# Up-projection bank by bank, and rounding, sine and gate of two banks one after the other in second halves

## The chip, the cores and the metric

The kernel runs on one core of one Trainium2 chip. The metric is the device time of one execution in microseconds; smaller is better. Of the engines, TensorE (PE) multiplies matrices into PSUM banks, VectorE (DVE), ScalarE (ACT) and GpSimd (POOL) work on tiles, and the SyncE queue (SP) issues most of the DMAs; ScalarE's queue issues a few.

## The reference

Two blocks, one behind the other. The first is an mLSTM cell over 4 batches, 8 heads, 768 steps and head size 40; the second takes its output as 3072 rows of 320 and computes `x @ w_in` (320 by 2048), then `h * cos(h)`, then a product with `w_out` (2048 by 320).

```python
for t in range(S):
    m_new = np.maximum(f_gate[:, :, t] + m, i_gate[:, :, t])
    f_stab = np.exp(f_gate[:, :, t] + m - m_new)
    i_stab = np.exp(i_gate[:, :, t] - m_new)
    m = m_new
    C = f_stab[:, :, None, None] * C + i_stab[:, :, None, None] * np.einsum('bhd,bhe->bhde', vt, kt)
    n = f_stab[:, :, None] * n + i_stab[:, :, None] * kt
    h_tilde = np.einsum('bhde,bhe->bhd', C, qt)
    denom = np.maximum(np.abs(np.einsum('bhd,bhd->bh', n, qt)[:, :, None]), 1.0)
    y[:, :, t] = h_tilde / denom / (1.0 + np.exp(-o_gate[:, :, t]))
...
h = x @ w_in
return ((h * np.cos(h)) @ w_out).astype(np.float32)
```

## The kernel before

The sequence is cut into 6 chunks (c) of 128 steps. A cell n = 4c + b is chunk c of batch b, with all 8 heads: 24 cells, n = 0 to 23. In a cell the scores (matrices k by q, line 485) are weighed by the decay on VectorE (`weigh`, 491), multiplied by the values (`values`, 511 to 520), normalised on VectorE (`normalize_turned`, 529 to 540; the last step writes `xT`, the input of the second block), and the state is brought up to date (`seam`, 603, puts the increments in PSUM; `state`, 628, adds them on VectorE in four instructions, two for each half of the partitions; `fade`, 586, on POOL; cells 20 to 23 have no such update). `seam_out` (610) copies the last 64 of the 320 features, which a cell leaves in `xT`, into `xL` by two DMAs that ScalarE's queue issues. The transposes of q and k for the next cell are two VectorE instructions (`turn_blocks`, 458), and the next scores wait for them; `scale_q` (467) and `weigh_k` (413) prepare further operands on POOL.

The second block works on a chunk whose cells are done. Its 2048 columns of `w_in` are taken in 8 parts (f2 = 0 to 7) of 256 columns, called halves here, since two of them go with one cell. `Up` (633) makes one: it takes two PSUM banks of 128 by 512 float32 (`pup`), one for each 128 columns (e = 0, 1), and fills each by three products: two of 128 rows (line 651) and one of 64 rows (line 645, `low`, from `xL`). The pool `ps_u` has two banks in all, so a half may write a bank only when the half before has finished reading it. In odd f2 of chunks 0 to 4 `low` is issued first, otherwise last. Then come four steps for each bank: `near` (659, ScalarE) rounds to int32, `rest` (662, VectorE) takes the remainder, `sin` (667, ScalarE) takes the sine of it, `gate` (671, VectorE) multiplies the sine by the bank. The result `g` goes to `sums` (720 to 723 on VectorE, 725 to 728 on POOL), which prepares a product with fewer multiplications, and that product with `w_out` is issued in `down_slot` (line 761, tiles `acc` and `late`; in chunk 0 line 683, tile `po`). At the second half that goes with the first cell of a chunk (n = 12, 16, 20), VectorE also has `combine` and `combine_late` (781 to 798) for the output of the chunk before.

The order is written out by hand, in one program order that every engine keeps for its own instructions (`manual_schedule`). `both_parts(c, b)` (966) issues a cell n = 4(c + 1) + b together with two halves of chunk c: the first (i = 0, even f2) with the scores ahead and `weigh` between `rest` and `sin`, then `down_slot`, `values`, `seam`, `normalize_turned`; the second (i = 1, odd f2) with `seam_out`, `state`, `sums`, then `down_slot`, and the preparations for cell n + 1. In chunk 5 there are halves but no cells. The first cells, 0 to 3, have an order of their own (`first_cells`).

In chunk 0 the weights are also converted, from 64-bit numbers to float32, between these steps: `take_apart` (154, 156) on ScalarE, `bound` (160, 161) and the first part of `put_together` (167) on VectorE, its last part (168) on POOL. A buffer of raw weights is free for the next load, issued on SP, only when its last step is done.

In second halves the order on ScalarE before was: near of both banks, the two DMA issues of `seam_out`, sine of both banks; and on VectorE: rest of both banks, the four instructions of `state`, gate of both banks, `sums`, the transposes.

Of the kernel before, what the change touches and what calls it, by code (L numbers as in the profile page):

```python
# [29 lines left out]
def kernel(  # L30
# [33 lines left out]
    NK = DM // 128  # L64
# [317 lines left out]
    def psum_o():  # L382
        return ps_o.tile([128, HP, C], FP, name="pm", tag="o")
# [6 lines left out]
    def decay_exponents(n):  # L390
        E = Es[n]
        if n < B:
            nc.vector.tensor_tensor(out=E, in0=E, in1=cols(n, 0, C), op=OP.subtract)
        nc.gpsimd.affine_select(out=E, in_=E, compare_op=OP.is_ge, fill=1.0e30, base=0,
                                pattern=[[0, H], [1, C]], channel_multiplier=-1)
# [45 lines left out]
    def clear_low():  # L441
        for w in "qk":
            nc.gpsimd.memset(raws[w][1], 0.0)
# [34 lines left out]
    def scores(n):  # L478
        pool, tag = psum(n)
        qT, kT = qkT[n]  # L480
        ps = [pool.tile([128, HP, C], FP, name="ps", tag=tag) for _ in range(2)]
        for p in range(HP):
            for j in range(2):
                r = slice(64 * j, 64 * j + D)
                nc.tensor.matmul(ps[j][:, p], kT[r, p], qT[r, p], start=True, stop=True)  # L485
        pss[n] = ps

    def weigh(n):
        for j in range(2):
            w = Es[n].rearrange("p (a j) t -> p a j t", j=2)[:, :, j]  # L490
            nc.vector.tensor_tensor(out=w, in0=pss[n][j], in1=w, op=OP.mult)  # L491
# [51 lines left out]
    def new_x(c):  # L543
        xT[c] = p2.tile([128, NK * B + 1, C], FP, name="xT", tag="xT")
        xL[c] = p2.tile([128, B, C], FP, name="xL", tag="xL")
# [20 lines left out]
    def halves(n):  # L566
        for j in range(2):
            r = slice(64 * j, 64 * j + D)
            for lo, hi, x in ((0, 32, HP * 32 * j), (32, DV, H * 32)):
                s = st[n % B][r, x:x + HP * 32].rearrange("q (p d) -> q p d", p=HP)  # L570
                yield j, r, s if lo == 0 else s[:, :, 16 * j:16 * j + 16], slice(lo, hi)

    def increment(n, r, w):
        u = pus[n][r, :, w]
        return u if w.start == 0 else u.rearrange("q p (o d) -> q p d o", o=2)

    def like(s, u):
        return s.rearrange("q p (d o) -> q p d o", o=2) if len(u.shape) == 4 else s
# [27 lines left out]
    def seam_out(n):  # L606
        c, b = divmod(n, B)
        if n >= B:
            for e in range(2):
                nc.scalar.dma_start(out=xL[c][64 * e:64 * e + 64, b], in_=ys[n][0:128:2])  # L610
            return
        if b == 0:
            new_x(c)
        nc.scalar.copy(out=xT[c][:, NK * b:NK * b + NK], in_=pxs[n][:, 0:NK])
        if b == B - 1:
            nc.vector.tensor_copy(out=xL[c][:, b], in_=pxs[n][:, NK])
        else:
            nc.scalar.copy(out=xL[c][:, b], in_=pxs[n][:, NK])

    def state(n):  # L620
        if n < N - B:
            for j, r, s, w in halves(n):
                u = increment(n, r, w)
                s = like(s, u)
                if n < B:
                    nc.scalar.copy(out=s, in_=u)
                else:
                    nc.vector.tensor_tensor(out=s, in0=s, in1=u, op=OP.add)
# [4 lines left out]
    class Up:  # L633


        def __init__(self, c, f2):
            self.c, self.f2 = c, f2
            self.pu = [ps_u.tile([128, B * C], FP, name="pup", tag="up") for _ in range(2)]

            ahead = f2 % 2 == 1 and c < NC - 1  # L640

            def low():
                for e, pu in enumerate(self.pu):
                    r = slice(64 * e, 64 * e + 64)
                    nc.tensor.matmul(pu, w_in_l[r, f2], xL[c][r].rearrange("p b t -> p (b t)"), start=ahead, stop=not ahead)  # L645

            if ahead:
                low()
            for i in range(NK):
                for e, pu in enumerate(self.pu):  # L650
                    nc.tensor.matmul(pu.rearrange("p (b t) -> p b t", b=B), w_in_sb[:, i, ts(2 * f2 + e, 128)], xT[c][:, i:NK * B:NK],  # L651
                                     start=(i == 0 and not ahead), stop=(i == NK - 1 and ahead))
            if not ahead:
                low()
            self.n = [p3.tile([128, B * C], I32, name="n", tag="n") for _ in range(2)]
# [174 lines left out]
    def warm(k, bank=None):  # L830

        for _ in range(k):
            nc.tensor.matmul(bank or pw, nil, nil.unsqueeze(1).to_broadcast([128, HP, 128]), start=True, stop=True)
# [132 lines left out]
    def both_parts(c, b):  # L966

        n = (c + 1) * B + b
        cell = n < N
        for i in range(2):  # L970
            f2 = 2 * b + i
            up = Up(c, f2)
            if cell and i == 0:
                scores(n)
                if c == 0 and b == 0:

                    warm(8, psum_o())
            if cell and i == 1:
                if n % 2 == 1 and n > B + 1 and n + 3 < N:
                    load_two(n + 3, "Kv")  # L980
            for e in range(2):
                up.near(e)
            for e in range(2):
                up.rest(e)
            if i == 0:
                if cell:
                    weigh(n)
                    if n + 1 < N:
                        decay_exponents(n + 1)
                    if n == B:  # L990
                        clear_low()
                for e in range(2):
                    up.sin(e)
                    up.gate(e)
                if c > 0:
                    sums(c, f2)
                if b == 0 and c == 1:
                    sigmoid(c + 1)

                if c == 0:  # L1000
                    next_out(*[pieces.pop(0) for _ in range(min(b, len(pieces), 1))])
                if cell and n + 1 < N:
                    decay(n + 1)
            else:
                if cell:
                    seam_out(n)
                if cell:
                    state(n)
                for e in range(2):
                    up.sin(e)  # L1010
                    up.gate(e)
                if c > 0:
                    sums(c, f2)
                if n == B + 1:
                    low_dimensions(n + 1)
                if c == 0:
                    next_out(*pieces)
                    pieces.clear()
                if cell and n + 1 < N:
                    if c > 0:  # L1020
                        weigh_k(n + 1)
                    odd_values(n + 1)
            if i == 1 and b == B - 1 and 0 < c < NC - 2:
                sigmoid(c + 2)
                sin_next()
            down_slot(c, f2)
            if f2 == 0 and c > 1:
                for p in range(2):
                    combine_first(c - 1, p)
            if cell and i == 0:  # L1030
                turn_gate(n)
                values(n)
                seam(n)
                normalize_turned(n)
                fade(n)
                if c == 1 and b < 3:
                    weight_sums(b + 1)
                if n % 2 == 1 and n > B + 1 and n + 3 < N:
                    load_two(n + 3, "qk")
                if n > B + 1 and n + 3 < N:  # L1040
                    load_E(n + 3)
                if b == B - 2 and c + 2 < NC:
                    load_o(c + 2)
                if c == 0 and pieces:
                    to_float32(pieces.pop(0))
                sin_next()
            if f2 == 0 and c > 1:
                for p in range(2):
                    combine(c - 1, p)
            if i == 1:  # L1050
                if c == 0 and b + 2 < B:
                    pieces.extend(weights_in(b + 2))
                    load_two((n + 3) // 2 * 2)
                    load_E(n + 3)
                if cell and n + 1 < N:
                    turn_blocks(n + 1)
                    scale_q(n + 1)
                    if c == 0:
                        weigh_k(n + 1)
                if (c, f2) == (0, LAST):  # L1060
                    weight_sums(0)
# [43 lines left out]
```

## Time and profile before

| | |
|---|---|
| time, median of 3 runs | 542.03 us (541.94 to 544.99) |
| span of the profiled execution | 541.8 us |
| TensorE busy | 518.0 us (96%) |
| VectorE busy | 420.1 us (78%) |
| ScalarE busy | 285.1 us (53%) |
| POOL busy | 227.0 us (42%) |
| mean granted TensorE clock | 0.980 of full speed |

The profile records one execution; its span runs from the first to the last instruction. A busy share is an average over stages with different limits: the first 50 us or so (first cells, loads), chunk 0 with the conversion of weights (to about 147 us), chunks 1 to 4 (to about 465 us), and chunk 5 with the last products. Costliest groups (busy in all, and one instruction):

| line | engine | what | number | busy us | one, ns |
|---|---|---|---|---|---|
| 651 | PE | pup, 128 rows | 384 | 178.4 | 607 |
| 645 | PE | pup, 64 rows | 192 | 54.3 | 642 |
| 659 | ACT | near | 96 | 53.6 | 593 |
| 662 | DVE | rest | 96 | 62.9 | 687 |
| 667 | ACT | sine | 96 | 57.7 | 628 |
| 671 | DVE | gate | 96 | 61.6 | 683 |

A float32 product is two instructions in the trace, here called passes, and the mean of one includes the overlap with its neighbours; from one start to the next of the 128-row passes is about 0.44 us. In the rows of a timeline, x2 says that two instructions are merged in one row, and the bracket gives the engine's idle time before it and what ended it.

### The profile page before, as it was taken

What the parts mean: (1) busy time and instruction counts of PE and PEld (TensorE: products, weight loads), DVE (VectorE), ACT (ScalarE), POOL (GpSimd) and SP (SyncE); (2) the same over time, 40 slices, a digit from 0 to 9 for tenths busy, and PEclk for the clock granted to TensorE, in tenths of its full rate; (3) what the DMA queues carried; (4) which work ended last, traced back from release to release, by engine and by line L of the source; (5) the groups of instructions that cost most, each with busy time, mean ns of one, the idle gap of its engine ahead of it and who ended that gap; (6) DMA issues with size and microseconds to landing.
All of it is one profiled execution on the core that took longest, in us unless ns stands there. A gap on an engine that the chain in (4) does not pass through costs nothing.

```text
span 541.8 us, 10496 instructions
## 1 busy us (share of the span) xinstructions
PE 518.0 (96%) x3844; PEld 349.5 (65%) x3844; DVE 420.1 (78%) x907; ACT 285.1 (53%) x546; POOL 227.0 (42%) x369
## 2 busy tenths in 40 slices
PE   7997889879999999999999999999999999999996
PEld 4874545545566666766767757757757767576755
DVE  5864978689688897898887898888898878673636
ACT  2876938496395355836436836526836522222221
POOL 7535354446376665434443533543422421221211
PEclk9968889999999999999999999999999999999999
DMA  9999759489677737519439329249320000010001
GB/s 137 209 199 222 220 151 214 131 164 246 137 124 178 104 94 168 63 68 208 46 95 189 41 82 198 44 107 178 38 93 7 2 5 6 10 41 1 0 1 48
DMA packets 99940, 57.81 MB, mean 107 GB/s; under 512 B 62305, under 2 KB 92609, under 8 KB 99889
## 3 DMA queue, kind: packets, MB, share of 16 engines
q1 hardware_dynamic: 96496, 55.64, 48.3%
q10 hardware_dynamic: 3248, 1.33, 1.2%
q8 instruction: 30, 0.49, 0.4%
q14 instruction: 22, 0.17, 0.1%
q0 software_dynamic: 144, 0.18, 0.1%
HBM read 51.71 MB, written 4.11 MB: 103 GB/s over the span
## 4 chain that ended last, share of the span: by engine, by line
PE 75%; DVE 9%; DMA 7%; POOL 2%; SPq 2%; ACT 2%; issue 2%; DVEq 0%; POOLq 0%; ACTq 0%
PE pup L651 27%; PE acc L761 23%; PE pup L645 8%; PE po L683 3%; PE ps L485 3%; PE late L761 3%; DMA E<-M_d 2%; PE vt L520 2%; DMA bits<-in_moe_w_in_dram 2%; PE vt L511 2%; DMA xL<-xT 1%; PE pu L603 1%; DVE g L671 1%; DMA vs<-in_v_dram 1%; SPq L330 1%
## 5 line engine op out<-in xcount | busy, mean ns | idle before, releaser
L651 PE MATMUL pup<-xT,w_in_sb 128*128 128x512 f32 x384 | 178.4, 607 | 5.2 <-DVE g L671 2.5
L659 ACT ACTIVATE n<-pup 128x512 int32<-128x512 f32 x96 | 53.6, 593 | 194.1 <-PE pup L645 142.6
L651 PEld LDWEIGHTS pup<-xT,w_in_sb 128*128 128x128 f32 x384 | 70.3, 192 | 93.0 <-issue 88.1
L662 DVE SCALAR_TENSOR_TENSOR n<-pup,n 128x512 f32<-128x512 f32 x96 | 62.9, 687 | 80.1 <-ACT n L659 78.7
L725 POOL TENSOR_TENSOR D<-g 128x128 f32<-128x128 f32 x40 | 19.9, 497 | 218.2 <-DVE g L671 218.2
L667 ACT ACTIVATE n<-n 128x512 f32<-128x512 f32 x96 | 57.7, 628 | 23.1 <-DVE n L662 15.4
L671 DVE SCALAR_TENSOR_TENSOR g<-pup,n 128x512 f32<-128x512 f32 x96 | 61.6, 683 | 3.9 <-ACT n L667 3.3
L761 PE MATMUL acc<-w_out_sb,g 128*128 128x160 f32 x320 | 58.6, 304 | 0.0
L761 PE MATMUL acc<-T,g 128*128 128x160 f32 x320 | 58.0, 301 | 0.1
L645 PE MATMUL pup<-xL,w_in_l 64*128 64x512 f32 x192 | 54.3, 642 | 1.3 <-POOL w_in_l L168 1.3
L761 PEld LDWEIGHTS acc<-w_out_sb,g 128*128 128x128 f32 x320 | 47.7, 190 | 5.6 <-issue 4.2
L761 PEld LDWEIGHTS acc<-T,g 128*128 128x128 f32 x320 | 48.1, 190 | 3.7 <-issue 3.0
L408 ACT ACTIVATE E<-E,tab 128x128 f32<-128x128 f32 x160 | 49.0, 389 | 0.3
L683 PE MATMUL po<-w_out_sb,g 128*128 128x320 f32 x128 | 36.4, 437 | 1.5 <-POOL w_out_sb L168 1.5
L761 PE MATMUL acc<-T,S 128*128 128x160 f32 x160 | 35.0, 300 | 0.0
L485 PEld LDWEIGHTS ps<-t,t 40*128 40x128 f32 x384 | 24.6, 188 | 12.5 <-DVE t L458 6.6
L683 PEld LDWEIGHTS po<-w_out_sb,g 128*128 128x128 f32 x128 | 23.8, 190 | 13.4 <-POOL w_out_sb L168 3.1
L645 PEld LDWEIGHTS pup<-xL,w_in_l 64*128 64x128 f32 x192 | 14.6, 186 | 25.1 <-issue 19.8
L491 DVE TENSOR_TENSOR E<-ps,E 128x512 f32<-128x512 f32 x48 | 30.6, 679 | 0.0
L761 PE MATMUL acc<-w_out_sb,S 128*128 128x160 f32 x160 | 28.8, 299 | 0.0
L958 ACT ACT_TABLE_LOAD x22 | 28.2, 1283 | 0.4
L761 PEld LDWEIGHTS acc<-T,S 128*128 128x128 f32 x160 | 26.2, 190 | 3.0 <-issue 3.0
(175 smaller groups left out, 878.8 us busy)
## 6 DMA issues: line engine op xcount, KB each, us to landing
E<-M_d SPq DMA_DIRECT2D x22, 512.0 KB
qr<-in_q_dram SPq DMA_DIRECT2D x36, 160.0 KB
kr<-in_k_dram SPq DMA_DIRECT2D x36, 160.0 KB
G<-G_d SPq DMA_DIRECT2D x20, 256.0 KB
bits<-in_moe_w_out_dram SPq DMA_DIRECT2D x8, 640.0 KB
bits<-in_moe_w_in_dram SPq DMA_DIRECT2D x32, 128.0 KB
out_dram<-o_sb SPq DMA_DIRECT2D x24, 160.0 KB
ks<-in_k_dram SPq DMA_DIRECT2D x10, 320.0 KB
```

What stands on the lines that cost most here:

```text
L408: nc.scalar.activation(out=Es[n][:, h], in_=Es[n][:, h], func=AF.Exp, scale=-1.0, bias=tab[:, c, 0, g:g + 1])
L485: nc.tensor.matmul(ps[j][:, p], kT[r, p], qT[r, p], start=True, stop=True)
L491: nc.vector.tensor_tensor(out=w, in0=pss[n][j], in1=w, op=OP.mult)
L645: nc.tensor.matmul(pu, w_in_l[r, f2], xL[c][r].rearrange("p b t -> p (b t)"), start=ahead, stop=not ahead)
L651: nc.tensor.matmul(pu.rearrange("p (b t) -> p b t", b=B), w_in_sb[:, i, ts(2 * f2 + e, 128)], xT[c][:, i:NK * B:NK], start=(i == 0 and not ...
L659: nc.scalar.activation(out=self.n[e], in_=self.pu[e], func=AF.Copy, bias=0.25)
L662: nc.vector.scalar_tensor_tensor(out=self.n[e].bitcast(FP), in0=self.pu[e], scalar=0.25, in1=self.n[e], op0=OP.add, op1=OP.subtract)
L667: nc.scalar.activation(out=r, in_=r, func=AF.Sin, scale=TWO_PI_DOWN)
L671: nc.vector.scalar_tensor_tensor(out=g, in0=self.pu[e], scalar=TWO_PI, in1=self.n[e].bitcast(FP), op0=OP.mult, op1=OP.mult)
L683: nc.tensor.matmul(po[c][b], gs[c, f][:, ts(b, C)], w_out_sb[:, f], start=(f == 0), stop=(f == NF - 1))
L761: nc.tensor.matmul(a, lhs, rhs, start=start, stop=stop)
L958: nc.scalar.activation(out=spot, in_=spot, func=AF.Sin)
```

## The change

Two edits. In `Up` the loops are exchanged: both 128-row products of the first bank are issued ahead of those of the second, in all halves. In `both_parts`, near and rest of both banks are now issued together only in first halves. In second halves `seam_out` comes first, then near, rest and sine of the first bank, near of the second, half of `state`, gate of the first bank, rest and sine of the second, the other half of `state`, gate of the second. `state` takes an argument for it that picks one half. The instructions are the same ones; on ScalarE the order becomes: two DMA issues, near, sine, near, sine; on VectorE: rest, two of `state`, gate, rest, two of `state`, gate. POOL and SP keep their order.

```diff
-    def state(n):
+    def state(n, only=None):
         if n < N - B:
             for j, r, s, w in halves(n):
+                if only not in (None, j):
+                    continue
                 u = increment(n, r, w)
...
-            for i in range(NK):
-                for e, pu in enumerate(self.pu):
+            for e, pu in enumerate(self.pu):
+                for i in range(NK):
                     nc.tensor.matmul(pu.rearrange("p (b t) -> p b t", b=B), w_in_sb[:, i, ts(2 * f2 + e, 128)], xT[c][:, i:NK * B:NK],
                                      start=(i == 0 and not ahead), stop=(i == NK - 1 and ahead))
...
-            for e in range(2):
-                up.near(e)
-            for e in range(2):
-                up.rest(e)
             if i == 0:
+                for e in range(2):
+                    up.near(e)
+                for e in range(2):
+                    up.rest(e)
                 if cell:
                     weigh(n)
...
             else:
                 if cell:
                     seam_out(n)
+                up.near(0)
+                up.rest(0)
+                up.sin(0)
+                up.near(1)
                 if cell:
-                    state(n)
-                for e in range(2):
-                    up.sin(e)
-                    up.gate(e)
+                    state(n, 0)
+                up.gate(0)
+                up.rest(1)
+                up.sin(1)
+                if cell:
+                    state(n, 1)
+                up.gate(1)
                 if c > 0:
                     sums(c, f2)
```

## The prediction

> **What bounds the kernel now.** I read the page's engine row and chain of waits, then the timelines of TensorE, VectorE and ScalarE over one cell of chunk 2, then the waits, then the stages before and after. The chain:
>
> ```profile
> PE 75%; DVE 9%; DMA 7%; POOL 2%; SPq 2%; ACT 2%; issue 2%; DVEq 0%; POOLq 0%; ACTq 0%
> ```
>
> From 126 to 526 us it runs through matmuls almost alone; before that, through weight loading and VectorE; after it, through the last half's rounding, sine and gate. So the price of the change is the TensorE idle time that it makes or removes. One cell (n = 14), TensorE, then VectorE, then ScalarE (start, length, what):
>
> ```profile
> 273.33 3.70 PE L651 MATMUL pup<-xT,w_in_sb 128*128 128x512 f32 x8
> ...
> 280.67 3.60 PE L651 MATMUL pup<-xT,w_in_sb 128*128 128x512 f32 x8
> 284.20 1.13 PE L645 MATMUL pup<-xL,w_in_l 64*128 64x512 f32 x4
> 285.16 1.06 PE L485 MATMUL ps<-t,t 40*128 40x128 f32 x16
> ```
>
> ```profile
> 275.26 0.56 DVE L540 TENSOR_TENSOR xT<-yt,db 128x384 f32<-128x384 f32 x1
> 276.90 1.49 DVE L662 SCALAR_TENSOR_TENSOR n<-pup,n 128x512 f32<-128x512 f32 x2 [1.08 <-ACT n L659]
> 278.31 0.86 DVE L628 TENSOR_TENSOR st<-st,pu 40x128 f32<-40x128 f32 x4
> 279.20 1.29 DVE L671 SCALAR_TENSOR_TENSOR g<-pup,n 128x512 f32<-128x512 f32 x2
> ...
> 282.96 1.07 DVE L458 STREAM_TRANSPOSE t<-kr 128x512 f32<-128x512 f32 x1
> ```
>
> ```profile
> 276.27 0.60 ACT L659 ACTIVATE n<-pup 128x512 int32<-128x512 f32 x1 [3.01 <-PE pup L651]
> 277.07 0.60 ACT L659 ACTIVATE n<-pup 128x512 int32<-128x512 f32 x1 [0.20 <-PE pup L651]
> 277.13 1.18 ACTq L610 DMA_DIRECT2D xL<-xT  x2
> 278.35 1.15 ACT L667 ACTIVATE n<-n 128x512 f32<-128x512 f32 x2 [0.69 <-DMA E<-M_d]
> ```
>
> See: TensorE has no gap. VectorE works without a gap from 276.90 to the end of the transposes, 284.03. The scores (L485), which need them, start at 285.16: 1.07 us of slack after 0.06 us of passing on. That slack is 1.37 in chunk 0's last cell, 0.6 in chunk 1, 1.07 in chunks 2 and 3, 0.64 in chunk 4, and 0 where combine runs (n = 12, 16, 20; transposes end 244.98, scores 245.03). A sine queued behind seam_out's DMA issues waits for them.
>
> **Part 1, product bank by bank.** Same instructions. A pass is 0.44 us (eight in 280.67 to 284.20). In second halves of chunks 0 to 4 the first bank is complete two passes (0.88) sooner, the second as now. In first halves, and in chunk 5, the 64-row products come last and nothing is complete sooner; but the second bank is first written 1.77 after the first, instead of 0.88, so it can be released 0.88 later. One loss: in half 2 of chunk 0 TensorE does four passes, then waits for the second weight block (72.63, idle 2.48, POOL L168). Now two are done and six remain: +0.88.
>
> **Part 2, seam_out ahead of near(0).** On ScalarE the two DMA issues (1.12 to 1.18) now stand before both roundings, and wait for xT (275.82). Nearest row: the one above, where the sine starts 0.04 after the issues end. So near(0) starts about 275.82 + 1.22 = 277.04: not 0.88 sooner (275.39), but 0.77 later than now. Bounds: 275.39 if the issue holds nothing back; 0.95 more if it lasts 2.07, as at 396.76. I take 1.22, the common length.
>
> **Part 3, one bank after the other.** ScalarE and VectorE now hand over in turn: near 0.60, rest 0.69, sine 0.62, gate 0.68, then rest, sine, gate of the second bank 0.69 + 0.62 + 0.68, with 0.17 of passing on: 4.75 from near(0) to the last gate, 4.12 from the first rest. The second rounding runs under the first gate. state's two pairs (0.43 each) lie under the sines: free. Last gate: 277.04 + 4.75 = 281.79, now 280.49: +1.30 (call it d). The first gate ends at 279.73, now 279.85: no gain. Behind the last gate on VectorE wait the sums and both transposes, behind those the scores. TensorE's second bank is needed only at 280.67 + 1.77 = 282.44: no wait (in chunk 1 by 0.2 to 0.3, at n = 20 0.2 too late, where the scores wait longer anyway). POOL's sums come d later too, ahead of weigh_k and scale_q; scale_q's output, ready at 285.03, is read at 290.39: covered. The order on POOL and SP is as it was; SP's q and k loads wait for the transposes, and what they bring is read a cell later or more. state ends some 1.8 later than 279.17; its PSUM tile is free before the scores need one.
>
> The same sum elsewhere (end of L540 + 5.97, against the last gate now) gives d = 1.21, 1.63, 1.64, 1.19 in chunk 1; 1.11 to 1.33 in chunks 2 and 3; 1.34 and 1.96 in chunk 4. In the combine cells VectorE is busy until the first rest, which hides part 2: 237.42 + 4.12 = 241.54 against 240.80, d = 0.74; in chunk 4, without state's 0.86 to save, 398.65 + 4.12 against 401.32, d = 1.45.
>
> **The sum, cells 8 to 23.** Let p be TensorE's lateness. VectorE's lateness x in a cell is p at its first-half product, or p at its scores less the 0.3 to 0.7 by which the normalisation (L529) now starts after the values end (0 at n = 21), if more. The next scores are late by x + d − slack, or by p if that is more. From zero at the scores of cell 8:
> chunk 1: 0.63, 1.16, 1.68, 1.76;
> chunk 2 (0.74 with no slack, then d about equal to the slack): 2.42, 2.42, 2.64, 2.64;
> chunk 3: 3.38, 3.38, 3.63, 3.63;
> chunk 4 (1.45 with no slack): 5.08, 5.78, 6.45.
> So +6.45.
>
> **Chunk 0.** Here weights are converted behind the sines:
>
> ```profile
> 72.63 3.49 PE L651 MATMUL pup<-xT,w_in_sb 128*128 128x512 f32 x4 [2.48 <-POOL w_in_sb L168]
> 95.26 3.67 PE L651 MATMUL pup<-xT,w_in_sb 128*128 128x512 f32 x8 [1.19 <-DVE g L671]
> 100.21 1.13 PE L645 MATMUL pup<-xL,w_in_l 64*128 64x512 f32 x4 [1.28 <-POOL w_in_l L168]
> 121.47 3.67 PE L651 MATMUL pup<-xT,w_in_sb 128*128 128x512 f32 x8 [1.34 <-DVE g L671]
> ```
>
> n = 4: near(0) is held by the table load anyway. The last sine ends 64.95 + 0.69 + 0.03 + 0.62 + 0.03 + 0.68 + 0.69 + 0.03 + 0.62 = 68.34, now 66.82. ScalarE's six conversion steps follow, VectorE's put_together and POOL's L168 come 1.37 later, and TensorE with part 1's 0.88 is 2.24 late. The next weight DMAs wait on SP for POOL's w_out_sb (issue 61.28, length 14.49), so they land 1.37 later too. n = 5: near(0) at 93.24 on that clock; first rest 93.82; the last sine 97.2, now 94.27: +2.95, passed through ScalarE, VectorE and POOL to w_in_l and the transposes (no slack: 101.53, 101.59). n = 6: the same adds 1.1: 4.1. n = 7: d 0.70 under 1.37: nothing. The 1.19 and 1.34 of gate wait shrink, but TensorE then waits for w_in_l and the scores. So +4.1; if the weights landed when they do now, +2.2.
>
> TensorE's idle stretch at 72.63 becomes about 4.9 us (69.2 to 74.0). An idle 3.88 before 55.63 is followed by a granted clock of 0.72 over 56 to 62, a loss of some 1.7 us. Here 1.8 more would be absorbed, since TensorE waits for w_in_l until +2.9 in the next cell. The Trainium skill, TensorE: Matmul & The Clock Gate, "What's actually happening", has the clock halve after an idle window of about 3.4 us. By that rule the sum gains nothing if the wait absorbs it, and an estimated 1.7 if not; the trace agrees with the rule after 3.88 us.
>
> **The tail.** Last half: near(0) 527.66, so the last gate ends 527.66 + 4.75 = 532.41 plus 0.05, now 531.05: +1.41, on the path, since the last 18 matmuls start 0.05 after L723 (533.26). Chunk 5's other second halves lie under 9 us of matmuls.
>
> Total: 4.1 + 6.45 + 1.41 = 12.0 on the span of 541.8, which stands 0.2 under the runs' median of 542.03: 554.0.
>
> **Rivals.**
> Issues hold nothing back: part 2 is free, near(0) starts 0.88 sooner, d is −0.34 in ordinary cells. Left are 3.9 in chunk 0, 0.74 + 0.74 + 1.45 in the combine cells, and the tail: +8.2, 550. For: near(1) at 277.07 and the issue at 277.13 run side by side. Against: the issue is ahead in program order now, and the sine behind it waited.
> Issues last 2.07, as once: 0.95 more in some eight cells (n = 5, 6, 8 to 11, 21, 22): 561.5. For: loads are in flight beside them. Against: 1.12 in nearly all cells.
> Clock lost in chunk 0 and not absorbed: 555.7.
> Not slower: the gate waits of n = 5 and 6 (1.19 + 1.34) go, since the first bank is released 0.55 sooner and the second needed 0.88 later; the tail's 1.41 stays: 540.7. It decides if ScalarE's weight steps end no later than now. Against: they stand behind the last sine, 1.1 to 1.5 later, and the slack of the scores is short in chunk 1.
> That the order stays as it was is excluded: the built instructions stand as the change says.
>
> **How the numbers follow.** Forecast 0.62, hidden issues 0.15, long issues 0.10, clock 0.05, not slower 0.08. Leaving out the last and the outer part of the long issues, the range is 547 (hidden issues, weights landing as now, 2.0 less, and 1 for the hand-overs) to 560. A percent is 5.4 us, about what a measurement here tells from no change. Slower by more: the first four less 0.03 at their low edge, 0.89; within: 0.09; faster: 0.02.
>
> **What would show it.** Right: L610 ahead of L659, near(0) 1.2 after L540; gates one by one, each behind its sine; new TensorE idle before L485 from transposes, 0.5 a cell in chunk 1 and 1.4 at n = 21; the wait for the second weight block in half 2 ending 1.4 later; tail +1.4. Wrong: near(0) at the first bank's end, L485 without idle, or weights converted at the old times.

## The result, and the profile after

The changed kernel takes 556.55 us in the median of 4 runs (554.37 to 558.52); the kernel before, on the same chip, 541.99 (541.86 to 544.99, 4 runs). The ratio is 1.0244, with a 95% interval of 1.0208 to 1.0279. The profiled run of the changed kernel took 555.36 us, its span is 553.6. So 1.8 us lie outside the span, and the same 1.7 to 1.9 lie there in nearly every run of every kernel of this study, the kernel before among them.

Lines behind 626 have moved by 2: near is L661, rest L664, sine L669, gate L673, the sums L722 to L725. First the engine row and the chain of waits of the changed kernel:

```profile
PE 524.9 (95%) x3844; PEld 351.5 (63%) x3844; DVE 420.6 (76%) x907; ACT 285.7 (52%) x546; POOL 227.0 (41%) x369
...
PE 52%; DVE 25%; ACT 10%; DMA 4%; issue 3%; SPq 2%; POOL 2%; ACTq 1%; DVEq 0%; POOLq 0%
```

TensorE's share of the chain has fallen from 75% to 52%, VectorE's has grown from 9% to 25% and ScalarE's from 2% to 10%: the hand-over between the two now sets the time of some stages. The waits say the same (engine, tile and line, whom it waits for: us in total, times, the longest):

```profile
ACT n L669 <- DVE n L664: 49.8, 71, 1.8
...
DVE g L673 <- ACT n L669: 22.1, 52, 0.8
...
PEld ps L485 <- DVE t L458: 18.6, 18, 2.5
...
PE ps L485 <- DVE t L458: 5.8, 9, 1.7
```

The waits of the sine on the remainder were 15.4 us before, those of the gate on the sine 3.3. Only the last line is lost time of TensorE: 5.8 us in nine places, where it was 1.1 in three. The line above it is for the same scores, but counts weight loads, which partly run beside earlier products.

The cell of n = 14 in the changed kernel, VectorE's timeline (start, length, what, in brackets the idle time before it):

```profile
279.58 0.56 DVE L540 TENSOR_TENSOR xT<-yt,db 128x384 f32<-128x384 f32 x1
282.03 0.69 DVE L664 SCALAR_TENSOR_TENSOR n<-pup,n 128x512 f32<-128x512 f32 x1 [1.89 <-ACT n L661]
...
283.42 0.69 DVE L673 SCALAR_TENSOR_TENSOR g<-pup,n 128x512 f32<-128x512 f32 x1 [0.38 <-ACT n L669]
284.02 0.68 DVE L664 SCALAR_TENSOR_TENSOR n<-pup,n 128x512 f32<-128x512 f32 x1
...
285.40 0.69 DVE L673 SCALAR_TENSOR_TENSOR g<-pup,n 128x512 f32<-128x512 f32 x1 [0.23 <-ACT n L669]
...
288.55 1.09 DVE L458 STREAM_TRANSPOSE t<-kr 128x512 f32<-128x512 f32 x1
```

and ScalarE's:

```profile
280.18 1.12 ACTq L610 DMA_DIRECT2D xL<-xT  x2
281.40 0.60 ACT L661 ACTIVATE n<-pup 128x512 int32<-128x512 f32 x1 [3.83 <-PE pup L653]
282.75 0.63 ACT L669 ACTIVATE n<-n 128x512 f32<-128x512 f32 x1 [0.76 <-DVE n L664]
283.29 0.58 ACT L661 ACTIVATE n<-pup 128x512 int32<-128x512 f32 x1
284.74 0.63 ACT L669 ACTIVATE n<-n 128x512 f32<-128x512 f32 x1 [0.87 <-DVE n L664]
```

xT is ready at 280.14, the two DMA issues follow, and the first near starts at 281.40: 1.26 later, though the page gives TensorE as its releaser. TensorE's eight passes start at 277.64 and take 3.70, so the first bank was complete before xT; what ended the wait was the issues. From there to the end of the last gate at 286.09 it is 4.69. VectorE, which had no gap here, now idles 2.50 us in this stretch.

TensorE's own timeline, rows picked: chunk 0, the scores of n = 21 and what follows them, the last products:

```profile
71.79 5.48 PE L653 MATMUL pup<-xT,w_in_sb 128*128 128x512 f32 x6 [5.62 <-POOL w_in_sb L168]
...
101.14 2.08 PE L647 MATMUL pup<-xL,w_in_l 64*128 64x512 f32 x4 [2.85 <-POOL w_in_l L168]
...
413.25 1.16 PE L485 MATMUL ps<-t,t 40*128 40x128 f32 x16 [1.72 <-DVE t L458]
414.34 0.81 PE L763 MATMUL acc<-w_out_sb,g 128*128 128x160 f32 x4
414.99 0.67 PE L763 MATMUL acc<-T,S 128*128 128x160 f32 x2
415.45 1.27 PE L763 MATMUL acc<-T,g 128*128 128x160 f32 x4
416.52 1.27 PE L763 MATMUL acc<-w_out_sb,S 128*128 128x160 f32 x4
...
544.11 0.54 PE L763 MATMUL acc<-T,S 128*128 128x160 f32 x2 [0.67 <-DVE S L723]
545.10 0.81 PE L763 MATMUL acc<-T,g 128*128 128x160 f32 x4 [0.46 <-DVE g L725]
```

The gate waits of chunk 0 (1.19 and 1.34) are gone, 0.27 at 65.07 apart. The wait for the second weight block has grown from 2.48 to 5.62, that for w_in_l from 1.28 to 2.85, and after both TensorE is slow: six passes in 5.48, where six at 0.44 would take about 2.7, and four small ones in 2.08 instead of 1.13. (In the kernel before, the four passes after the wait of 2.48 were slow as well: 3.49, at a granted clock of 0.50.) New is the wait of 1.72 at n = 21, with four products in 1.27 behind it instead of 0.71. Where the time was lost, against the kernel before: the first row is taken at the end of n = 4's last write of `xT`, just ahead of the first changed second half (the scores of n = 4 start at nearly the same time in both, 48.91 and 48.86), the later rows at the start of each cell's scores.

| stretch | lateness gained, us | prediction |
|---|---|---|
| first cells, to `xT` of n = 4 | -2.12 | 0 |
| chunk 0, to the scores of n = 8 | 3.96 | 4.1 |
| chunk 1, to n = 12 | 1.88 | 1.76 |
| chunk 2, to n = 16 | 0.91 | 0.88 |
| chunk 3, to n = 20 | 1.03 | 0.99 |
| chunk 4, to n = 23 | 4.67 | 2.82 |
| tail | 1.48 | 1.41 |
| sum, the difference of the spans | 11.8 | 12.0 |

The first cells differ by up to 3.6 us between the profiles here, so lateness below is counted from this write of `xT` in n = 4. One value stands out, chunk 4.

### The profile page after: what moved, and what is told of

Its sections match the earlier page's. It is cut to its first block, busy times and chain, and to the rows that moved or that the text cites. A ratio compares the mean times of both kernels' runs of the same rounds, so it can differ in the third digit from the quotient of the medians.

```text
span 553.6 us, 10495 instructions
## 1 busy us (share of the span) xinstructions
PE 524.9 (95%) x3844; PEld 351.5 (63%) x3844; DVE 420.6 (76%) x907; ACT 285.7 (52%) x546; POOL 227.0 (41%) x369
## 4 chain that ended last, share of the span: by engine, by line
PE 52%; DVE 25%; ACT 10%; DMA 4%; issue 3%; SPq 2%; POOL 2%; ACTq 1%; DVEq 0%; POOLq 0%
PE pup L653 18%; PE acc L763 17%; PE pup L647 5%; DVE n L664 4%; DVE g L673 4%; DVE t L458 4%; ACT n L669 3%; PE ps L485 3%; PE po L685 2%; ACT n L661 2%; PE vt L520 2%; PE vt L511 1%; PE late L763 1%; DVE S L723 1%; DVE S L724 1%
## 5 line engine op out<-in xcount | busy, mean ns | idle before, releaser
L653 PE MATMUL pup<-xT,w_in_sb 128*128 128x512 f32 x384 | 180.5, 612 | 5.9 <-POOL w_in_sb L168 5.6
L661 ACT ACTIVATE n<-pup 128x512 int32<-128x512 f32 x96 | 54.3, 591 | 183.8 <-PE pup L647 117.0
L664 DVE SCALAR_TENSOR_TENSOR n<-pup,n 128x512 f32<-128x512 f32 x96 | 63.8, 685 | 71.5 <-ACT n L661 71.5
L669 ACT ACTIVATE n<-n 128x512 f32<-128x512 f32 x96 | 59.6, 630 | 49.8 <-DVE n L664 49.8
L673 DVE SCALAR_TENSOR_TENSOR g<-pup,n 128x512 f32<-128x512 f32 x96 | 64.0, 687 | 22.1 <-ACT n L669 22.1
L685 PE MATMUL po<-w_out_sb,g 128*128 128x320 f32 x128 | 37.6, 449 | 0.0
L485 PE MATMUL ps<-t,t 40*128 40x128 f32 x384 | 28.0, 287 | 5.9 <-DVE t L458 5.8
```

The costliest lines, as they stand in the source:

```text
L661: nc.scalar.activation(out=self.n[e], in_=self.pu[e], func=AF.Copy, bias=0.25)
L664: nc.vector.scalar_tensor_tensor(out=self.n[e].bitcast(FP), in0=self.pu[e], scalar=0.25, in1=self.n[e], op0=OP.add, op1=OP.subtract)
L669: nc.scalar.activation(out=r, in_=r, func=AF.Sin, scale=TWO_PI_DOWN)
L673: nc.vector.scalar_tensor_tensor(out=g, in0=self.pu[e], scalar=TWO_PI, in1=self.n[e].bitcast(FP), op0=OP.mult, op1=OP.mult)
L685: nc.tensor.matmul(po[c][b], gs[c, f][:, ts(b, C)], w_out_sb[:, f], start=(f == 0), stop=(f == NF - 1))
```

## The experiments

Each is measured against the kernel before on the same chip: 542.51 for seam_between, banks_only, order_only and chunk0_as_before, 541.97 for seam_front, tail_as_before, fill_21 and fill_chunk0, 542.59 for fill_weights, seam_late and seam_late_b.

**seam_between**: the changed kernel with the DMA issues behind the second near.

```diff
-                if cell:
-                    seam_out(n)
                 up.near(0)
                 up.rest(0)
                 up.sin(0)
                 up.near(1)
+                if cell:
+                    seam_out(n)
```

> The changed kernel with one move: in second halves seam_out's two DMA issues go behind near(1), where ScalarE waits for the second remainder anyway. Theory (the DMA issues ahead of near(0), and the one-by-one hand-over, both push the transposes and so the scores): near(0) starts some 2.1 us sooner after xT's last write (from 1.25 after it to the end of the first bank), the waits of the scores in chunk 1 (0.36, 0.37, 0.21) go, those at n = 13 and 17 stay near 0.7, n = 21 stays over 1.4, the tail stays. About 552.3 us, 4 less than the changed kernel's 556.5. Rival (the hand-over alone carries the loss, the issues are hidden): 556.5, chunk 1's waits stay. Rival (it gives everything back): 542.

Measured: 552.79 us (552.45 to 554.05), ratio 1.0187 (1.0162 to 1.0211), 3.8 less than the changed kernel. ScalarE in the cell of n = 14:

```profile
281.01 0.60 ACT L661 ACTIVATE n<-pup 128x512 int32<-128x512 f32 x1 [2.15 <-PE pup L653]
282.37 0.63 ACT L669 ACTIVATE n<-n 128x512 f32<-128x512 f32 x1 [0.76 <-DVE n L664]
282.75 0.47 ACTq L610 DMA_DIRECT2D xL<-xT  x1
282.90 0.58 ACT L661 ACTIVATE n<-pup 128x512 int32<-128x512 f32 x1
```

The issue at 282.75 starts beside the sine and the second near, and here it holds neither back: behind a running instruction it is hidden, ahead of the first one it is not. Chunks 1 to 4 cost 2.90 instead of 8.49; chunk 1 costs 0.20. Not all of the 5.59 is the issues' price: 1.67 of it is the lower clock behind the wait at n = 21 (fill_21 below), which did not come in this profile, though the wait is there (1.73). What is left is three steps of 0.65, 0.68 and 1.36, one for each combine cell (the scores of n = 13, 17, 21). That is the price of the alternation where VectorE is late into the first rounding.

**banks_only**: the kernel before with the loop exchange alone.

```diff
-            for i in range(NK):
-                for e, pu in enumerate(self.pu):
+            for e, pu in enumerate(self.pu):
+                for i in range(NK):
```

> The kernel before with the exchanged product loops alone. Theory: no loss outside chunk 0. In half 2 of chunk 0 six passes instead of four follow the wait for the second weight block, 0.9 us, and up to 2.7 if the longer idle stretch lowers the granted clock; the next cell's wait for w_in_l (1.28 before) takes up most of it: 542 to 543.5 us. Rival (the bank order is a cost of its own, as the product is the bulk of TensorE's work): a third or more of the loss, 547 us or more.

Measured: 544.49 us (541.15 to 545.18, 10 runs), ratio 1.0017 (0.9996 to 1.0037): no difference that can be told from none, though the median is 1.0 above the range expected. In its profile the wait for the second weight block is 3.46 instead of 2.48, with its six passes in 4.39, the gate wait of 1.19 has shrunk to 0.64, and no lateness is gained from n = 8 on.

**order_only**: the changed kernel with the old order of the products; near, rest, sine and gate as changed.

```diff
-            for e, pu in enumerate(self.pu):
-                for i in range(NK):
+            for i in range(NK):
+                for e, pu in enumerate(self.pu):
```

> The changed kernel with the product loops as before (both banks in turn), all else as changed. Theory: the second bank is needed 0.88 us sooner than with bank by bank, so the late second gate now also holds back the first-half product: new waits of 0.3 us a cell in chunks 2 and 3 and 0.8 to 1 in chunks 1 and 4 ahead of L651: 559 to 563 us, slower than the changed kernel. Rival (bank order makes no difference once the scores wait for the transposes): 556.5. Rival (bank by bank is part of the loss): below 555.

Measured: 560.51 us (557.92 to 563.06), ratio 1.0324 (1.0282 to 1.0366). TensorE's timeline in chunks 1 and 2:

```profile
189.73 2.81 PE L653 MATMUL pup<-xT,w_in_sb 128*128 128x512 f32 x6 [0.89 <-DVE g L673]
...
291.59 2.81 PE L653 MATMUL pup<-xT,w_in_sb 128*128 128x512 f32 x6 [0.25 <-DVE g L673]
```

Two passes run, then the second bank is awaited from the late last gate. Bank by bank it is needed two passes later, and these waits do not appear: alone the loop exchange is worth nothing, beside the new order it saves 4.0.

**seam_front**: the kernel before with only the DMA issues moved ahead of both nears.

```diff
+            if cell and i == 1:
+                seam_out(n)
             for e in range(2):
                 up.near(e)
...
             else:
                 if cell:
-                    seam_out(n)
-                if cell:
                     state(n)
```

> The kernel before, with only seam_out's DMA issues put ahead of both roundings in second halves; all else as before. Counted as the prediction counts it: near(0) starts 1.22 after xT, both rests follow, then state, then both gates; the last gate 0.78 later than before in ordinary cells, which the slack of the scores (1.07, 0.6 in chunk 1 and 0.64 in chunk 4) mostly hides. So 2 to 3 us more than the kernel before, 544.5 to 545 us. Rival (the issues cost the same in either order, 3.7, which is what moving them back saved in the changed kernel): 546.2. Second rival (the issues hold nothing back without the alternation): 542.5.

Measured: 547.29 us (546.75 to 548.3), ratio 1.0085 (1.0053 to 1.0116): 5.3 more than the kernel before, more than either theory. Its profile from n = 4 on is 4.7 later at the end, 3.5 of it in chunk 1. TensorE there:

```profile
163.91 3.67 PE L651 MATMUL pup<-xT,w_in_sb 128*128 128x512 f32 x8 [0.58 <-DVE g L671]
...
183.77 3.67 PE L651 MATMUL pup<-xT,w_in_sb 128*128 128x512 f32 x8 [0.70 <-DVE g L671]
...
204.18 3.67 PE L651 MATMUL pup<-xT,w_in_sb 128*128 128x512 f32 x8 [1.24 <-DVE g L671]
```

The expectation looked at the scores' slack. What ended last was the release of the first bank: near(0) is 1.26 behind xT, and the next half's products, which start 6.9 us after this half's where nothing holds them (156.27 and 163.20 in the kernel before), wait for the first gate. In the changed kernel that gate is early, since it no longer waits for the second rounding. So the issues cost much the same in both orders, through different waits: 5.3 in the old one by the medians and 4.7 by the profile; in the new one 3.8 by the medians, and by the profiles from n = 4 on 6.3, or 4.6 without the clock's 1.67.

**chunk0_as_before**: both edits off in chunk 0.

```diff
-            for e, pu in enumerate(self.pu):
-                for i in range(NK):
+            for e, i in ([(e, i) for i in range(NK) for e in range(2)] if c == 0 else [(e, i) for e in range(2) for i in range(NK)]):
...
+                if c == 0:
+                    for e in range(2):
+                        up.near(e)
+                    for e in range(2):
+                        up.rest(e)
+                    if cell:
+                        seam_out(n)
+                    if cell:
+                        state(n)
+                    for e in range(2):
+                        up.sin(e)
+                        up.gate(e)
+                else:
...
```

> The changed kernel with both edits left out in chunk 0 (loops and order of second halves as before there). Theory: chunk 0's part of the loss, about 4 us, goes: 552.5 us; the wait for the second weight block in half 2 is 2.5 again instead of 5.6, and the scores of cell 8 start at 147.6 after the start as before, give or take the 2 us by which the first cells differ from run to run. Rival (chunk 0's loss is taken up by its waits for weights): 556.5.

Measured: 554.15 us (552.63 to 555.02), ratio 1.0213 (1.0185 to 1.0241). Chunk 0 now gains 0.5 instead of 3.96 (the scores of n = 8; the wait for the second weight block is 2.88), chunks 1 to 4 gain 8.51 as in the changed kernel: the two prices are separate. The medians differ by only 2.4, less than the profiles say; the first cells' spread is in both.

**tail_as_before**: the old order of rounding, sines and gates in chunk 5 alone, with the products bank by bank. The branch is that of chunk0_as_before, under another condition:

```diff
-                if c == 0:
+                if c == NC - 1:
```

> The changed kernel, with the old order of rounding, sines and gates in chunk 5 only (no seam_out and no state is there); products bank by bank everywhere. Theory (the last half's last gate is later by the hand-overs, and nothing hides it): 1.4 to 1.5 less than the changed kernel, some 555.1 us, and TensorE's two waits in the last products (0.67 and 0.46) fall to the 0.35 of the kernel before. Rival (the second bank's later release costs the tail, not the order): no change, 556.5, and the waits stay.

Measured: 555.98 us (555.32 to 556.82), ratio 1.0244 (1.0212 to 1.0276). The median fell by 0.6 only, within the spread, but the profile shows the term: it is 11.7 late at the scores of n = 23 and 11.8 at the end, so the tail costs 0.1 instead of 1.5, and neither of the two waits in the last products is left.

**fill_21**: the changed kernel, with TensorE kept busy in the 1.72 of n = 21.

```diff
+        if n == 21:
+            for _ in range(7):
+                nc.tensor.matmul(ps[0], nil, nil.unsqueeze(1).to_broadcast([128, HP, 128]), start=True, stop=True)
         for p in range(HP):
             for j in range(2):
```

> The changed kernel, with seven idle matmuls of a zero tile written into the scores' own bank just ahead of the scores of n = 21, where TensorE waits 1.72 us for the transposes; the scores write over them. Theory (the wait itself costs 1.72, and the half clock after it another 1.67): the products behind those scores take 0.71 for four instead of 1.27, and the time falls by 1.7, to some 554.9 us. Rival (the half clock there has another cause than the wait, and comes now and then): the rows stay at 1.27 and the time at 556.5, or the clock is low at another place.

Measured: 554.87 us (554.01 to 557.72), ratio 1.0232 (1.0191 to 1.0272). TensorE's timeline:

```profile
412.63 1.69 PE L484 MATMUL ps<-nil 128*128 128x512 bf16 x7
414.52 1.16 PE L488 MATMUL ps<-t,t 40*128 40x128 f32 x16 [0.21 <-DVE t L458]
415.61 0.81 PE L766 MATMUL acc<-w_out_sb,g 128*128 128x160 f32 x4
416.26 0.43 PE L766 MATMUL acc<-T,S 128*128 128x160 f32 x2
416.53 0.71 PE L766 MATMUL acc<-T,g 128*128 128x160 f32 x4
417.08 0.71 PE L766 MATMUL acc<-w_out_sb,S 128*128 128x160 f32 x4
```

The scores are as late as before (the filling takes the place of the wait), the products behind them run at full length, and from n = 8 to n = 23 the lateness gained is 6.82 instead of 8.49: 1.67 less. The granted clock of the changed kernel, by windows (from and to, length, five engines' busy times with counts, clock, DMA share, GB/s), shows what went:

```profile
414.00:415.00 1.00, 1.00 (x13) 0.88 (x10) 0.80 (x2) 0.98 (x3) 0.73 (x1) 1.00 0.00 0
415.00:416.00 1.00, 1.00 (x7) 1.00 (x6) 1.00 (x3) 1.00 (x1) 0.00 (x0) 0.53 0.00 0
416.00:417.00 1.00, 1.00 (x5) 1.00 (x5) 0.99 (x2) 0.99 (x4) 0.00 (x0) 0.50 0.00 0
417.00:418.00 1.00, 1.00 (x5) 1.00 (x5) 0.00 (x0) 1.00 (x4) 0.46 (x1) 0.50 0.00 0
418.00:419.00 1.00, 1.00 (x8) 1.00 (x7) 0.00 (x0) 0.98 (x4) 0.00 (x0) 0.77 0.00 0
```

Half speed from 415 to some 418.5, though TensorE was busy again from 413.25.

**fill_chunk0** and **fill_weights**: the same filling in chunk 0. The first had 24 of the products in half 1, which has no such wait, and its profile shows them delaying the work of that half: near(0) of n = 4 stands 4.37 behind xT instead of 1.24. It says nothing on the clock's price. The second, with its edit:

```diff
                 for i in range(NK):
+                    if (c, f2, e, i) == (0, 2, 0, 1):
+                        warm(24, ps_a.tile([128, HP, C], FP, name="pm", tag="a"))
...
             if not ahead:
+                if (c, f2) == (0, 4):
+                    warm(12, ps_a.tile([128, HP, C], FP, name="pm", tag="a"))
                 low()
```

> The changed kernel, with 24 idle matmuls in the wait for the second weight block (half 2 of chunk 0, 5.62 us) and 12 in the wait for w_in_l in half 4 (2.85 us). The six passes after the first wait should take 2.7 instead of 5.5, and w_in_l's products after the second 1.13 instead of 2.08. Theory (the prediction's: the half clock in chunk 0 is absorbed by later waits for weights): at most 0.5 less than the changed kernel, 556.0 to 556.5 us; the wait for w_in_l in half 4 grows by what is saved before it. Rival (the half clock reaches the end): 1.7 or more less, 554.8 us or below.

> The changed kernel, with 24 idle matmuls of a zero tile in the wait for the second weight block (half 2 of chunk 0, 5.62 us) and 12 in the wait for w_in_l in half 4 (2.85 us), in a bank of the scores' pool; the earlier run of this kind had the 24 in half 1, where there is no such wait. The six passes after the first wait should take 2.7 us instead of 5.5, w_in_l's products after the second 1.13 instead of 2.08. Theory (the prediction's: the half clock in chunk 0 is absorbed by later waits for weights): at most 0.5 less than the changed kernel, 556.0 to 556.5 us. Rival (the half clock reaches the end): 1.7 or more less, 554.8 us or below.

Measured: fill_chunk0 560.32 us (559.67 to 561.21), ratio 1.0328 (1.0291 to 1.0366); fill_weights 555.81 us (554.62 to 557.91), ratio 1.0225 (1.0187 to 1.0263). TensorE in the second:

```profile
69.56 5.34 PE L839 MATMUL pm<-nil 128*128 128x512 bf16 x24
75.41 2.84 PE L655 MATMUL pup<-xT,w_in_sb 128*128 128x512 f32 x6 [0.51 <-POOL w_in_sb L168]
...
101.29 2.75 PE L839 MATMUL pm<-nil 128*128 128x512 bf16 x12
104.58 1.13 PE L647 MATMUL pup<-xL,w_in_l 64*128 64x512 f32 x4 [0.53 <-POOL w_in_l L168]
```

Both stretches are at full speed, and chunk 0 costs 4.06 instead of 3.96: what the clock takes there, later waits give back. In this profile the wait at n = 21 is 1.72 again, unfilled, and no slow products follow.

**seam_late** and **seam_late_b**: an order without the two prices. Products bank by bank (in the second one not in chunk 0), in chunk 5's odd halves with the 64-row products first; second halves as follows:

```diff
-            ahead = f2 % 2 == 1 and c < NC - 1
+            ahead = f2 % 2 == 1
...
-                if cell:
-                    seam_out(n)
                 up.near(0)
                 up.rest(0)
-                up.sin(0)
                 up.near(1)
                 if cell:
                     state(n, 0)
-                up.gate(0)
                 up.rest(1)
+                up.sin(0)
+                up.gate(0)
                 up.sin(1)
-                if cell:
-                    state(n, 1)
                 up.gate(1)
+                if cell and (c > 0 or b == B - 1):
+                    seam_out(n)
+                if cell:
+                    state(n, 1)
...
                     pieces.clear()
+                    if cell and b < B - 1:
+                        seam_out(n)
```

> Products bank by bank as in the changed kernel (in chunk 5's odd halves with the 64-row products first), but in second halves near(0), rest(0), near(1), state's first pair, rest(1), sin(0), gate(0), sin(1), gate(1), and seam_out's issues only behind them (in chunk 0 behind the weight conversions too, but for its last cell). Theory (the issues ahead of the roundings, and the second rounding behind the first sine and gate, are the whole price): the last gate is about 1.2 earlier than in the kernel before, TensorE does not wait for transposes or gates, and chunk 0's weights come 0.5 to 1 earlier: 540 to 541.5 us, 0.5 to 2 less than the kernel before. Rival (bank by bank itself costs in chunk 0, by the half clock after the longer wait for the second weight block): 543 to 545.

> As seam_late, but with the old order of the products in chunk 0. Theory (bank by bank costs in chunk 0, where the weights come late, and is free elsewhere): 540 to 541.5 us, and at most 0.5 above seam_late or up to 1.5 below it. Rival (in chunk 0 the earlier first bank is worth more than the longer wait): 0.5 to 1 above seam_late.

Measured: seam_late 544.23 us (542.98 to 546.2, 12 runs), ratio 1.0024 (1.0004 to 1.0044); seam_late_b 543.38 (542.36 to 546.54, 12 runs), ratio 1.0015 (0.9993 to 1.0036). So the price of the change goes almost whole, but nothing is won: both miss the 540 to 541.5 expected, and seam_late lies in the range of its rival, the cost of bank by bank in chunk 0. From n = 4 on the profile of seam_late is 1.8 later than the kernel before's at n = 23: 1.0 in chunk 0, where the wait for the second weight block is 3.68 and its six passes take 4.28, and 0.5 at each of the first two combine cells, which wait 0.76 and 0.74 for the transposes. There VectorE works without a gap in both kernels, so moving `state` changes almost nothing: at n = 12 it is 6.95 against 6.88 from the start of `xT`'s last write to the first of the sums. Most of the 0.5 is the four sums, which take 1.81 instead of 1.41 up to the next instruction; the last of them alone takes 0.54 instead of 0.28. Why it is slower is not shown. In the other cells the last gate is 0.3 to 0.8 earlier, counted from `xT` (1.2 expected), and hardly any lateness falls: TensorE had no wait there to lose. No order tried is faster than the kernel before.

## Why the prediction came out right

The forecast was 554.0, the measurement 556.55; the mechanism is the predicted one.

- **Bank by bank.** Free by itself (banks_only). That TensorE would not wait for the second bank, since it is needed 0.88 later, held too; order_only shows what this is worth: 4.0 us.
- **Issues ahead of near(0).** 1.22 predicted between xT and near, 1.24 to 1.26 measured in ordinary cells (1.40 and 1.44 in two). The rivals on both sides, issues that hold nothing back and issues of 2.07, fall by that row. Moving the issues saves 3.8 by the medians, so the rival with hidden issues (4.0 below the forecast) had the price about right and the fact wrong.
- **One bank after the other.** 4.75 predicted from near(0) to the last gate, 4.69 measured in ordinary cells. Counted from `xT`, the last gate is 1.19, 1.80, 1.62 and 1.17 later in chunk 1, where 1.21, 1.63, 1.64 and 1.19 were predicted.
- **The sum over cells.** Lateness gained since n = 8, predicted and measured, is 1.76 and 1.88 at n = 12, 2.64 and 2.79 at n = 16, 3.63 and 3.82 at n = 20, 5.08 and 5.19 at n = 21. At n = 23 it is 6.45 against 8.49, and 6.82 with the wait filled. So the step that failed is the assumption that TensorE's lateness at n = 21 passes on as it is: the wait of 1.72 was counted as some 1.4 of idle time alone, and it also halved the clock for 3.4 us, which cost 1.67 more. That the clock fell there in the profiled run is partly chance: two other profiles have the same wait and keep the clock.
- **Chunk 0.** 4.1 predicted, 3.96 measured; the weight block of half 2 came 1.28 later, counted from `xT` of n = 4, where 1.37 was predicted. Part of the agreement is luck, since the steps inside differ: 3.12, 3.54, 3.96 and 3.96 late at the scores of n = 5 to 8, predicted 2.24, 2.95, 4.1 and 4.1. The first is larger because the six passes behind the longer wait ran at half clock, so that the two more cost 1.99 (5.48 less 3.49) and not 0.88. The prediction's own row, four passes in 3.49 behind the wait of 2.48, showed the half clock there already; it took the wait of 3.88 as its only example. That the loss is absorbed was right (fill_weights). So the prediction looked for a cost of the clock here, where it has none in the end, and not at n = 21, where it has.
- **The tail.** 1.41 predicted, 1.48 measured; with the old order it is 0.1.
- **The sum.** 4.1 + 6.45 + 1.41, on the kernel before's median, is 554.0. The reason given for the last 0.2 is not right: 1.8 us of a run lie outside the span, so the profiled span of 541.8 belongs to a run of about 543.6 and not of 542.03; but the terms are differences, and the total comes to the median plus 12.0 all the same. (The rival that is not slower is 540.9 by the same count, not 540.7.) Measured, the medians differ by 14.6. The profiled run gives 3.96 + 6.82 + 1.48 + 1.67 = 13.93 for it, with the clock's term last, and the rest lies within the spread of the first cells.
- **Not slower.** The gate waits did go, but the weights came later, as the prediction said against this rival.

## What to carry to other kernels

An instruction that merely starts a DMA still takes its place in its engine's queue: put behind a running instruction it can be free, put at the head of a chain that hands work to another engine it delays the whole chain, here by 1.7 us at n = 14 (near(0) starts 1.26 after `xT` instead of 0.44 ahead of it), since the issues first wait for their own input. Alternating two engines on one bank at a time releases the first buffer sooner and makes the last result later, so look first at which of the two is awaited. And price a new wait of the matrix engine above its own length: what follows may run at half clock, as it did in 4 profiles of 6 after 1.72 us, and whether that reaches the end depends on a later wait that can take it up.

## What the runs showed of the hardware that was not expected

A wait of 1.72 us was enough to halve TensorE's clock. Six profiles have the same wait of 1.72 or 1.73 unfilled before the scores of n = 21: behind it the clock fell in four of them (the changed kernel, chunk0_as_before, tail_as_before, fill_chunk0) and not in two (seam_between, fill_weights). In the changed kernel the lower clock began 1.8 us after the wait had ended (415.05 against 413.25), and lasted 3.4 us.

What told the four from the two can be read from the clock records: in each of the 13 profiles all changes of the clock lie whole multiples of 3.413 us apart, to 0.001 us. Laid on this grid, 1.61 to 1.72 us of the wait fall into one step of 3.413 in the four profiles where the clock was halved from the next step on; in seam_between it is 1.57, and in fill_weights the wait is split into 1.09 and 0.64. A wait of 3.66 before the second weight block of seam_late_b, split into 1.74 and 1.92, left the clock at 1.00. So where a wait falls on the grid counts as well as its length; how much of a step has to be idle is not settled by these numbers.

The Trainium skill, TensorE: Matmul & The Clock Gate, section "What's actually happening", tells of an activity window of about 3.4 us that runs freely, and of half the clock after an idle one. The grid agrees with such a window; that a whole window must be idle does not, since 1.61 of 3.41 was enough here.
